# Attention block on one core: ones in every eighth column of the value tiles, and the next keys at an earlier tile count

## The chip, the core and the metric

The kernel runs on one core of a Trainium2 chip. The metric is the device time of one execution in microseconds (us): 416.04 us, the median of three runs (415.42 to 416.15). The core has a matrix engine (PE, TensorE), a vector engine (DVE, VectorE), an activation engine (ACT, ScalarE), a general engine (POOL, GpSimd) and an engine that here only issues DMAs (SP, SyncE). Each runs its own instructions in the order in which the program holds them and waits on semaphores for the others. PE writes to PSUM, eight banks of 128 x 512 floats; the other data lie in SBUF.

## The reference, cut to what matters

```python
B, S, D, H = 1, 2048, 448, 16          # Dh = 28
qkv = (x @ wqkv).reshape(B, S, 3, H, Dh).transpose(2, 0, 3, 1, 4)
q, k, v = qkv
scores = einsum("bhqd,bhkd->bhqk", q, k) * Dh ** -0.5
o = einsum("bhqk,bhkd->bhqd", softmax(scores), v)
return o.transpose(0, 2, 1, 3).reshape(B, S, D) @ wo
```

All in bfloat16. The bulk is 16 heads x 2048 x 2048 exponentials.

## The kernel before, in words

**Tiling.** The 16 heads form four groups g of four; the 2048 queries form four chunks c of 512. A pair (g, c) is a window; 16 windows run one after the other, group by group. In a window there are 16 rows of 128 keys, each with four score tiles, one a head, of 128 keys x 512 queries: 64 tiles a window, 256 a group, 1024 in all. `pos` counts the score tiles started. A head takes 32 partitions or columns (HP), of which 28 carry data. Scores are computed transposed (keys on the partitions), so that the exponentials go straight into the product with the values.

**Score tile.** `emit_S` (L865) multiplies a block of keys (KB) with the queries (QB). The stationary operand spans 64 partitions, two heads' strips: one strip of 32 holds the head's data, the other holds in KB a row of key maxima (the bound) and in QB the absolute queries, so that a bound on the scores is subtracted within the matmul. The bound makes the exponentials safe without a maximum over the scores.

**Exponentials.** Three engines share them. ACT takes two tiles at a time out of a double bank PA into PTA (L1288). DVE takes single tiles out of one of three banks PD: DU (L1069), DV (L1072), then POOL's product DG (L1075), then DVE's sum PTD (L1088). A few tiles ("g") are copied to SG by DVE (L1001) and worked off by POOL alone (L1008 to L1031); such a tile is chosen 10 to 13 rows ahead.

**Values.** `pv_op` (L1133) multiplies the 32 value columns of a head (VA) with the exponentials and adds up over the 16 rows of a window in the one bank PO. Of the 32 columns 28 are values and the last four are ones (L317, L450), so that partitions 28 to 31 of each head's strip of PO hold the softmax denominators.

**End of a window.** `finish_window` (L944): PO is copied to OSB (L953); one denominator row a head, four rows, is gathered by a DMA into DCO, 128 x 16 (L960); DVE inverts it into DRC (L962); a DMA writes it to DRAM as four rows of 512 (SCR, L963); a DMA reads each row 32 times into the 128 partitions of RRB (L965); POOL multiplies OSB by RRB into OT (L968). The last window is normalized on DVE instead, by transposes (`norm_dve`, L876). OT of all four groups goes through the output projection with WO (L789, L807, L827, L899, L1420), which has its rows laid out as the heads' strips (L445).

**First two windows.** Their first four rows run before the bound of all keys is known, with a bound from the first chunk; `task_factor` (L906) computes the ratio exp(old bound - new bound) into RR, writes eight of its rows to DRAM (SCRF, L930), broadcasts them into RRB (L931), and `finish_block` rescales the first part by them (L941).

**Work for the next group.** While group g-1 runs, its tasks are woven in. `task_K` (L509): for each chunk sc of 512 keys four matmuls (L523), an eviction into KB on DVE (L558) and a maximum (L562). Chunk sc may start from tile (g-1)*256 + sc*KSP + 2 (L519); it takes the bank PO when no window holds it, and any free bank PD from (sc+1)*KSP - UK on (L518). After all four chunks, `task_kmax` (L568) reduces the maxima (L572), builds the bound tile NK on POOL (L616), copies two strips of keys into the second KB tile (KB<-KB, L604) and writes the bound beside each head's keys (KB<-NK, four DMAs, L614). `task_Q` (L628) makes the queries of a window about one window ahead and lays them out with six DMAs (L701, L707). `task_V` (L714) makes VA and evicts it on DVE (L739).

**Order.** The order of every engine is fixed at build time by a planner in the kernel (from L1324 on). It steps through modelled time; each operation has an engine, a duration, a latency until others see it, dependencies, a priority and perhaps a tile count from which it is eligible. On PE, score matmuls for ACT come first, then those for DVE, then the value matmuls once enough rows are ready (10 at the start of a window), then the tasks. DMAs count 0.4 to 0.6 us on SP; GLAT is the modelled time from there until the broadcast RRB has landed, and so sets where in POOL's order the multiply by RRB stands. The chip then keeps that order and waits wherever a semaphore isn't there yet. The priority of the multiply and of the DMAs of the end of a window is -10, ahead of the tiles'.

Of the kernel before, what the change touches and what calls it, by code (L numbers as in the profile page):

```python
# [10 lines left out]
ALU = mybir.AluOpType  # L11
# [3 lines left out]
F32 = mybir.dt.float32  # L15
# [3 lines left out]
P = 128  # L19
H = 16  # L20
HP = 32
G = 4
HG = 4
CC = 4
QW = 512
# [57 lines left out]
def kernel(  # L83
# [7 lines left out]
    nc = tc.nc  # L91
    _, S, D = x.shape
    Dh = D // H
# [3 lines left out]
    TPC = QW // P  # L97
    SCALE = float(Dh) ** -0.5
    YSC = 128.0 / LN2 * SCALE
    GW = HG * Dh  # L100
# [12 lines left out]
    NG = 3  # L113
    GMAX = 1
    UK = 30
    KSP = 64
    PGX = 0
    GDEC = 4
    LA = 10
# [18 lines left out]
    PFIN = 0.3  # L138
    QEA = 20
    PLT = 6.0  # L140
    GLAT = 6.5
    J3 = 9
    UQ = 60
    OD = 2
# [18 lines left out]
    NF = 2  # L163
# [41 lines left out]
    def sb(shape, dt, name):  # L205
        return const.tile(shape, dt, name=name)
# [5 lines left out]
    WO = sb([P, G, D], BF16, "WO")  # L212
# [32 lines left out]
    PA = [psum.tile([P, UA * QW], F32, name=f"PA{i}") for i in range(NA)]  # L245
# [84 lines left out]
    def add(op):  # L330
        static[op.eng].append(op)
        return op
# [108 lines left out]
        add(Op("SP", 8.5, None, prio=-1995.5))  # L441

    def load_wo():
        for i in range(HG):
            nc.sync.dma_start(out=WO[HP * i:HP * i + Dh, :, :],  # L445
                              in_=bass.AP(wo.tensor, wo.offset + i * Dh * D, [[D, Dh], [HG * Dh * D, G], [1, D]]))

    def va_ones():
        for g in range(1, G):
            nc.gpsimd.memset(VA[g][:].rearrange("p j h e -> p (j h) e")[:, :, Dh:HP], 1.0)  # L450
    add(Op("POOL", 0.9, va_ones, prio=-50, elig=lambda t: pos[0] >= 8))

    def halves():
        nc.gpsimd.memset(negm[:], 0.0)
        nc.gpsimd.memset(FW[:], 0.0)
        for w in range(NF):
            cs = slice(w * HP // NF, (w + 1) * HP // NF)
            nc.gpsimd.tensor_scalar(out=negm[:, w, cs], in0=maskm[:, cs], scalar1=-1.0, scalar2=0.0, op0=ALU.mult, op1=ALU.add)
    add(Op("POOL", 0.8, halves, prio=-49, elig=lambda t: pos[0] >= 8))
    add(Op("SP", 1.7, load_wo, prio=-500, elig=lambda t: pos[0] >= 110))  # L460
    for s in a_slots + d_slots + [o_slot]:
        s.free_at = 1e18

# [250 lines left out]
    def task_V(g, jq):  # L714
        due = g * 4 * WT + jq * TPC * HG - 12 + (FB * HG * (NF - 1) if g == 0 and jq else 0)
        task = bank_task()
        early = False
        elig = at(VE + jq * 5 if g == 0 else (g - 1) * 4 * WT + jq * WT + 4)
        prio = due
        ap = lambda: bank(task)[:]  # L720

        def mm(jj):
            for cc in range(CC):
                nc.tensor.matmul(out=ap()[:, jj * GW:(jj + 1) * GW], lhsT=XT[jq][cc // 2][0:CK, cc % 2, jj * P:(jj + 1) * P],  # L724
                                 rhs=WV[:, cc, g * GW:(g + 1) * GW], start=(cc == 0), stop=(cc == CC - 1))
        ops = []
        for jj in range(TPC):
            ops.append(add(Op("PE", 0.27, (lambda jj=jj: mm(jj)), deps=(xt_done[jq] + [wvin]) if jj == 0 else [ops[-1]],
                              prio=prio + 0.001 * jj, kind="W", elig=elig, acq=acq_d(task, early, urgent=due - UV if g == 0 else (g - 1) * 4 * WT + (jq + 1) * WT + 32) if jj == 0 else None,
                              lat=0.0 if jj < TPC - 1 else PLAT)))  # L730
        o = VA[g][:, jq * TPC:(jq + 1) * TPC, :, 0:Dh]
        eng = "ACT" if early else "DVE"

        def ev_fn():
            src = ap()[:, 0:TPC * GW].rearrange("p (j h d) -> p j h d", j=TPC, d=Dh)
            if eng == "ACT":
                nc.scalar.copy(out=o, in_=src)
            else:
                nc.vector.tensor_copy(out=o, in_=src)  # L739
# [165 lines left out]

    def task_factor():  # L906
        task = bank_task()
        hh = HP // NF

        def cut():  # L910
            for w in range(NF):
                for pr in range(2):
                    nc.gpsimd.tensor_copy(out=FW[:, w * 2 + pr, w * hh:(w + 1) * hh], in_=KB[0][pr][:, QW + w * hh:QW + (w + 1) * hh])

        def mm(w):
            for i in range(HG):
# [7 lines left out]
        for w in range(NF):  # L924
# [19 lines left out]
    def finish_window(w, pvop):  # L944
# [11 lines left out]
        def rel(t):  # L956
# [5 lines left out]
        o2 = add(Op("DVE", 0.17, lambda: nc.vector.reciprocal(out=DRC[b][:], in_=DCO[b][:]), deps=o1, prio=-4000))  # L962
        o3 = add(Op("SP", 0.4, lambda: nc.sync.dma_start(out=SCR[b][:].rearrange("i (a b) -> (i a) b", b=TPC * HG),  # L963
                                                         in_=DRC[b][:]), deps=[o2], prio=-10, lat=2.0))
        o4 = [add(Op("SP", 0.6, lambda: nc.sync.dma_start(  # L965
            out=RRB[b][:], in_=bass.AP(SCR[b][:].tensor, SCR[b][:].offset, [[QW, HG], [0, HP], [1, QW]])),
            deps=[o3], prio=-10, lat=GLAT))]
        o5 = add(Op("POOL", 1.22, lambda: nc.gpsimd.tensor_tensor(out=OT[g][c][:], in0=OSB[b][:], in1=RRB[b][:], op=ALU.mult),  # L968
                    deps=o4, prio=-10, kind="n"))
# [487 lines left out]
```

## Time and profile before

| what | value |
| --- | --- |
| median of three runs | 416.04 us (415.42 to 416.15) |
| profiled execution, first to last instruction | 417.6 us |
| PE busy | 360.6 us, 86% |
| DVE busy | 378.0 us, 91% |
| ACT busy | 395.7 us, 95% |
| POOL busy | 339.2 us, 81% |
| DMA packets, bytes | 36447, 16.58 MB |

The profile shows one execution. Its own time is the span from the first to the last instruction, 417.6 us, 0.4% over the median of the runs. A group's line names the source line, the engine, the operation, what it writes and reads with shapes, the count, then busy time and mean duration of one, then the idle time just before its instructions and what ended most of that. In tables of stretches each engine has its busy microseconds and the number of its instructions; PEclk is the share of the full clock that TensorE was granted. In the timeline the idle time before an instruction and its releaser stand in brackets.

### The profile page before, as it was taken

To read this page: it belongs to the slowest core of one execution; us is meant where nothing else is said; L and a number is where in the kernel's file an instruction comes from. 1 tells how busy PE (TensorE), PEld (TensorE's weight loads), DVE (VectorE), ACT (ScalarE), POOL (GpSimd) and SP (SyncE) were. 2 spreads that over 40 slices of the span, in tenths; PEclk is the share of its full clock that TensorE was granted. 3 is DMA by queue.
4 is the path that set the end of the run, shared out by engine and by line. 5 is a ranking of instruction groups with operands and counts; after the bars stand their busy time and mean duration, and the time that the engine had idled before them with its cause. 6 is when DMAs were issued, how large, how long until landed. Compare 5 with 4: busy or idle time off the path is not lost.

```text
span 417.6 us, 7577 instructions
## 1 busy us (share of the span) xinstructions
PE 360.6 (86%) x2591; PEld 118.8 (28%) x2604; DVE 378.0 (91%) x664; ACT 395.7 (95%) x434; POOL 339.2 (81%) x365
## 2 busy tenths in 40 slices
PE   7999989898798979788598897989898898889995
PEld 4343232223123222322213222232322222222321
DVE  6996999999689999999858999999999999999884
ACT  4999999999699999999869999999999999999993
POOL 4048999687678999998877899898989989999960
PEclk9999999999799999999969999999999999999999
DMA  9351130203300001110500101000140000010112
GB/s 211 49 85 44 36 74 6 48 5 75 67 1 27 19 29 29 20 35 5 104 17 2 36 12 34 14 28 19 29 94 3 26 20 27 2 39 9 67 49 89
DMA packets 36447, 16.58 MB, mean 40 GB/s; under 512 B 28785, under 2 KB 33137, under 8 KB 36409
## 3 DMA queue, kind: packets, MB, share of 16 engines
q1 hardware_dynamic: 35800, 15.89, 16.3%
q8 instruction: 20, 0.33, 0.3%
q10 hardware_dynamic: 608, 0.22, 0.2%
q14 instruction: 19, 0.15, 0.1%
HBM read 7.44 MB, written 1.97 MB: 23 GB/s over the span
## 4 chain that ended last, share of the span: by engine, by line
ACT 52%; PE 25%; DVE 8%; issue 7%; DMA 5%; POOL 2%; SPq 1%; DVEq 0%; ACTq 0%; POOLq 0%
ACT PTA L1288 51%; PE PA L865 10%; PE PO L1133 8%; PE PD L865 3%; DMA KB<-NK 2%; DVE DU L1069 2%; DVE DV L1072 1%; DMA KB<-KB 1%; DMA WK<-in_wqkv_dram 1%; DVE PTD L1088 1%; POOL DG L1075 1%; PE PO L523 1%; DVE QB L679 1%; DVE XT L426 1%; DVE KB L550 0%
## 5 line engine op out<-in xcount | busy, mean ns | idle before, releaser
L1288 ACT ACTIVATE PTA<-PA 128x1024 bf16<-128x1024 f32 x422 | 388.3, 1190 | 9.0 <-PE PA L865 8.2
L1075 POOL TENSOR_TENSOR DG<-DV,DU 128x512 f16<-128x512 f16 x155 | 177.3, 1156 | 38.1 <-DVE DV L1072 31.8
L865 PE MATMUL PA<-QB,KB 64*128 64x512 bf16 x843 | 170.9, 384 | 42.1 <-ACT PTA L1288 39.6
L865 PEld LDWEIGHTS <-KB 64*128 64x128 bf16 x1024 | 65.7, 93 | 187.7 <-issue 173.6
L1069 DVE TENSOR_SCALAR DU<-PD 128x512 f16<-128x512 uint16 x155 | 103.1, 682 | 10.8 <-PE PD L865 10.2
L1088 DVE SCALAR_TENSOR_TENSOR PTD<-PD,DG 128x512 uint16<-128x512 f32 x155 | 104.1, 682 | 4.5 <-POOL DG L1075 4.0
L1072 DVE SCALAR_TENSOR_TENSOR DV<-PD,DU 128x512 f16<-128x512 uint16 x155 | 103.5, 683 | 0.9
L1133 PE MATMUL PO<-PTA,VA 128*32 128x512 bf16 x843 | 88.4, 396 | 0.1
L865 PE MATMUL PD<-QB,KB 64*128 64x512 bf16 x181 | 65.0, 387 | 6.3 <-DMA KB<-NK 5.4
L1133 PE MATMUL PO<-PTD,VA 128*32 128x512 bf16 x181 | 51.7, 396 | 0.3 <-issue 0.3
L1133 PEld LDWEIGHTS <-VA 128*32 128x32 bf16 x1024 | 19.4, 94 | 52.4 <-issue 52.0
L1018 POOL TENSOR_TENSOR SG<-SG,GU 128x512 f32<-128x512 f32 x26 | 30.1, 1158 | 3.3 <-DVE PTD L1088 2.5
L1014 POOL TENSOR_TENSOR GV<-GE,GU 128x512 f16<-128x512 f32 x26 | 30.1, 1157 | 2.1 <-DVE DU L1069 0.9
L1016 POOL TENSOR_TENSOR GU<-GV,GU 128x512 f16<-128x512 f16 x26 | 30.1, 1156 | 1.2 <-DVE QP L692 0.5
L1001 DVE COPY SG<-PD 128x512 f32<-128x512 f32 x26 | 17.8, 685 | 10.8 <-PE PD L865 10.5
L1008 POOL TENSOR_SCALAR GU<-SG 128x512 f16<-128x512 uint16 x26 | 16.1, 621 | 9.3 <-DVE SG L1001 7.6
L968 POOL TENSOR_TENSOR OT<-OSB,RRB 128x512 bf16<-128x512 f32 x15 | 19.1, 1271 | 3.6 <-DVE QP L692 2.2
L1031 POOL TENSOR_SCALAR PTD<-SG 128x512 uint16<-128x512 f32 x26 | 16.2, 621 | 5.1 <-DVE QP L692 3.4
L653 PE MATMUL PO<-XT,WQP 112*128 112x512 bf16 x56 | 18.8, 386 | 0.4 <-DVE KB L550 0.4
L1011 POOL TENSOR_SCALAR GE<-SG 128x512 f32<-128x512 uint16 x26 | 16.1, 621 | 2.3 <-DVE QP L692 0.4
L724 PEld LDWEIGHTS <-XT 112*128 112x128 bf16 x256 | 13.4, 98 | 11.2 <-issue 10.9
L523 PE MATMUL PO<-XT,WKP 112*128 112x512 bf16 x48 | 15.4, 385 | 0.0
(108 smaller groups left out, 189.1 us busy)
## 6 DMA issues: line engine op xcount, KB each, us to landing
RRB<-SCR SPq DMA_DIRECT2D x15, 256.0 KB
QB<-QP SPq DMA_DIRECT2D x56, 32.0 KB
KB<-NK SPq DMA_DIRECT2D x12, 128.0 KB
XS<-in_x_dram SPq DMA_DIRECT2D x3, 448.0 KB
QB<-QB SPq DMA_DIRECT2D x28, 32.0 KB
out_dram<-XS SPq DMA_DIRECT2D x2, 448.0 KB
KB<-KB SPq DMA_DIRECT2D x6, 128.0 KB
RRB<-SCRF SPq DMA_DIRECT2D x2, 256.0 KB
```

What stands on the lines that cost most here:

```text
L523: ops = chain_mm(CC, lambda cc: nc.tensor.matmul(out=ap(), lhsT=WKP[g][:, cc, :], rhs=XT[sc][cc // 2][0:CK, cc % 2, :], start=(cc == 0), s ...
L865: nc.tensor.matmul(out=ap, lhsT=KB[g % 2][i // 2][a:a + 64, j * P:(j + 1) * P], rhs=QB[w % NQB][i // 2][a:a + 64, :], start=True, stop=Tru ...
L968: o5 = add(Op("POOL", 1.22, lambda: nc.gpsimd.tensor_tensor(out=OT[g][c][:], in0=OSB[b][:], in1=RRB[b][:], op=ALU.mult), deps=o4, prio=-10 ...
L1014: g3 = add(Op("POOL", PTT, lambda: nc.gpsimd.tensor_tensor(out=GV[:], in0=GE[:], in1=GU[:], op=ALU.mult), deps=[g2], prio=prio + 2, kind=" ...
L1016: g4 = add(Op("POOL", PTT, lambda: nc.gpsimd.tensor_tensor(out=GU[:], in0=GV[:], in1=GU[:], op=ALU.mult), deps=[g3], prio=prio + 3, kind=" ...
L1018: g5 = add(Op("POOL", PST, lambda: nc.gpsimd.tensor_tensor(out=X[:], in0=X[:], in1=GU[:], op=ALU.add), deps=[g4], prio=prio + 4, kind="g", ...
L1069: p1 = add(Op("DVE", P1, lambda: nc.vector.tensor_scalar(out=DU[b][:], in0=lo, scalar1=SIG / 65536, scalar2=SIG * (SS - 0.5), op0=ALU.mult ...
L1072: p2 = add(Op("DVE", P1, lambda: nc.vector.scalar_tensor_tensor(out=DV[b][:], in0=lo, scalar=65536 * (SS - 0.5 + CE / C3), in1=DU[b][:], o ...
L1075: gq = add(Op("POOL", PTT, lambda: nc.gpsimd.tensor_tensor(out=DG[b][:], in0=DV[b][:], in1=DU[b][:], op=ALU.mult), deps=[p2], prio=n, kind ...
L1088: f = add(Op("DVE", P1, lambda: nc.vector.scalar_tensor_tensor(out=PTD[st["s"].idx][:].bitcast(U16), in0=PX[slot.idx][:], scalar=EBITS + C ...
L1133: nc.tensor.matmul(out=PO[HP * st:HP * (st + 1), :], lhsT=VA[g][:, j, st, :], rhs=r["p"][i][1](), start=first, stop=last, tile_position=(0 ...
L1288: nc.scalar.activation(out=PTA[pslot.idx][:, 0:len(ns) * QW], in_=PA[s.idx][:, 0:len(ns) * QW], func=ACT.Exp, bias=ACT_BIAS, scale=ACT_SCALE)
```

## The change

Three things. **The ones** move from the last four columns of each head's 32 to every eighth column (RS = 8): seven values, a one, seven values, a one. So PO has its denominators at partitions 7, 15, 23, ..., 127, each head's four times; the gather takes 16 rows (NR), the reciprocal is over 128 x 64, SCR is 16 x 512, and the broadcast reads 16 rows eight times each. The value evictions write runs of 7; WO has its rows spread accordingly and is loaded in seven DMAs, not four; `norm_dve` reads column 7. **The rescale factors** RR get the same layout, each of the two windows having four of each eight columns, and go from RR in SBUF straight to RRB; SCRF is gone. **Two constants of the planner**: KSP 64 to 52, GLAT 6.5 to 2.4 (and the modelled durations of the load of WO, 1.7 to 2.9, and of the reciprocal, 0.17 to 0.22).

```diff
+RS = 8
+NR = 128 // RS
...
-    KSP = 64
+    KSP = 52
...
-    GLAT = 6.5
+    GLAT = 2.4
...
-    DCO = [sb([P, TPC * HG], F32, f"DCO{i}") for i in range(2)]
-    DRC = [sb([P, TPC * HG], F32, f"DRC{i}") for i in range(2)]
+    DCW = QW * NR // P
+    DCO = [sb([P, DCW], F32, f"DCO{i}") for i in range(2)]
+    DRC = [sb([P, DCW], F32, f"DRC{i}") for i in range(2)]
...
-    SCRF = dram.tile([HG, NF, QW], F32, name="SCRF")
-    SCR = [dram.tile([HG, QW], F32, name=f"SCR{i}") for i in range(2)]
+    SCR = [dram.tile([NR, QW], F32, name=f"SCR{i}") for i in range(2)]
...
+    def cols_of(ap, w):
+        f = RS // NF
+        return ap.rearrange("p (m e) -> p m e", e=RS)[:, :, w * f:(w + 1) * f]
+
+    def va_rows(g):
+        return VA[g][:].rearrange("p j h (m e) -> p (j h m) e", e=RS)
...
-    nc.vector.memset(VA[0][:].rearrange("p j h e -> p (j h) e")[:, :, Dh:HP], 1.0)
+    nc.vector.memset(va_rows(0)[:, :, RS - 1:RS], 1.0)
...
-        for i in range(HG):
-            nc.sync.dma_start(out=WO[HP * i:HP * i + Dh, :, :],
-                              in_=bass.AP(wo.tensor, wo.offset + i * Dh * D, [[D, Dh], [HG * Dh * D, G], [1, D]]))
+        for e in range(RS - 1):
+            nc.sync.dma_start(out=WO[e::RS, :, :],
+                              in_=bass.AP(wo.tensor, wo.offset + e * D, [[(RS - 1) * D, NR], [HG * Dh * D, G], [1, D]]))
...
-        o = VA[g][:, jq * TPC:(jq + 1) * TPC, :, 0:Dh]
+        nv = TPC * HG * HP // RS
+        o = va_rows(g)[:, jq * nv:(jq + 1) * nv, 0:RS - 1]
...
-        nc.vector.reciprocal(out=dr, in_=dt[:, Dh::HP])
+        nc.vector.reciprocal(out=dr, in_=dt[:, RS - 1::HP])
...
-        d = add(Op("SP", 0.5, lambda: nc.sync.dma_start(out=SCRF[:].rearrange("i w q -> (i w) q"), in_=RR[0::hh, :]), deps=[e], prio=-10, lat=2.0))
         return [add(Op("SP", 0.6, lambda w=w: nc.sync.dma_start(
-            out=RRB[w][:], in_=bass.AP(SCRF[:].tensor, SCRF[:].offset + w * QW, [[NF * QW, HG], [0, HP], [1, QW]])),
-            deps=[d], prio=-10, lat=GLAT)) for w in range(NF)]
+            out=RRB[w][:], in_=RR[w * RS // NF::RS, None, :].to_broadcast([NR, RS, QW])), deps=[e], prio=-10, lat=GLAT)) for w in range(NF)]
...
-            out=DCO[b][:], in_=OSB[b][Dh::HP, :].rearrange("i (a b) -> i a b", b=TPC * HG)), deps=[ev], prio=-10, lat=2.6))]
-        o2 = add(Op("DVE", 0.17, lambda: nc.vector.reciprocal(out=DRC[b][:], in_=DCO[b][:]), deps=o1, prio=-4000))
-        o3 = add(Op("SP", 0.4, lambda: nc.sync.dma_start(out=SCR[b][:].rearrange("i (a b) -> (i a) b", b=TPC * HG),
+            out=DCO[b][:], in_=OSB[b][RS - 1::RS, :].rearrange("i (a b) -> i a b", b=DCW)), deps=[ev], prio=-10, lat=2.6))]
+        o2 = add(Op("DVE", 0.22, lambda: nc.vector.reciprocal(out=DRC[b][:], in_=DCO[b][:]), deps=o1, prio=-4000))
+        o3 = add(Op("SP", 0.4, lambda: nc.sync.dma_start(out=SCR[b][:].rearrange("i (a b) -> (i a) b", b=DCW),
                                                          in_=DRC[b][:]), deps=[o2], prio=-10, lat=2.0))
...
-            out=RRB[b][:], in_=bass.AP(SCR[b][:].tensor, SCR[b][:].offset, [[QW, HG], [0, HP], [1, QW]])),
+            out=RRB[b][:], in_=bass.AP(SCR[b][:].tensor, SCR[b][:].offset, [[QW, NR], [0, RS], [1, QW]])),
             deps=[o3], prio=-10, lat=GLAT))]
```

The weights of the factor matmuls (FW, negm) are cut by `cols_of` in place of halves of the 32 columns; their shapes stay.

More of the change, by code (lines that the diff above doesn't have):

```diff
@@ L443, in load_wo @@
     def load_wo():
-        for i in range(HG):
-            nc.sync.dma_start(out=WO[HP * i:HP * i + Dh, :, :],
-                              in_=bass.AP(wo.tensor, wo.offset + i * Dh * D, [[D, Dh], [HG * Dh * D, G], [1, D]]))
+        for e in range(RS - 1):
+            nc.sync.dma_start(out=WO[e::RS, :, :],
+                              in_=bass.AP(wo.tensor, wo.offset + e * D, [[(RS - 1) * D, NR], [HG * Dh * D, G], [1, D]]))
     def va_ones():
         for g in range(1, G):
-            nc.gpsimd.memset(VA[g][:].rearrange("p j h e -> p (j h) e")[:, :, Dh:HP], 1.0)
+            nc.gpsimd.memset(va_rows(g)[:, :, RS - 1:RS], 1.0)
     add(Op("POOL", 0.9, va_ones, prio=-50, elig=lambda t: pos[0] >= 8))
@@ L456, in halves @@
         for w in range(NF):
-            cs = slice(w * HP // NF, (w + 1) * HP // NF)
-            nc.gpsimd.tensor_scalar(out=negm[:, w, cs], in0=maskm[:, cs], scalar1=-1.0, scalar2=0.0, op0=ALU.mult, op1=ALU.add)
+            nc.gpsimd.tensor_scalar(out=cols_of(negm[:, w, :], w), in0=maskm[:, 0:HP // NF].rearrange("p (m f) -> p m f", f=RS // NF),
+                                    scalar1=-1.0, scalar2=0.0, op0=ALU.mult, op1=ALU.add)
     add(Op("POOL", 0.8, halves, prio=-49, elig=lambda t: pos[0] >= 8))
-    add(Op("SP", 1.7, load_wo, prio=-500, elig=lambda t: pos[0] >= 110))
+    add(Op("SP", 2.9, load_wo, prio=-500, elig=lambda t: pos[0] >= 110))
     for s in a_slots + d_slots + [o_slot]:
@@ L730, in task_V @@
                               lat=0.0 if jj < TPC - 1 else PLAT)))
-        o = VA[g][:, jq * TPC:(jq + 1) * TPC, :, 0:Dh]
+        nv = TPC * HG * HP // RS
+        o = va_rows(g)[:, jq * nv:(jq + 1) * nv, 0:RS - 1]
         eng = "ACT" if early else "DVE"
         def ev_fn():
-            src = ap()[:, 0:TPC * GW].rearrange("p (j h d) -> p j h d", j=TPC, d=Dh)
+            src = ap()[:, 0:TPC * GW].rearrange("p (n e) -> p n e", e=RS - 1)
             if eng == "ACT":
@@ L907, in task_factor @@
         task = bank_task()
-        hh = HP // NF
         def cut():
@@ L912, in cut @@
                 for pr in range(2):
-                    nc.gpsimd.tensor_copy(out=FW[:, w * 2 + pr, w * hh:(w + 1) * hh], in_=KB[0][pr][:, QW + w * hh:QW + (w + 1) * hh])
+                    nc.gpsimd.tensor_copy(out=cols_of(FW[:, w * 2 + pr, :], w),
+                                          in_=KB[0][pr][:, QW:QW + HP // NF].rearrange("p (m f) -> p m f", f=RS // NF))
         def mm(w):
```

## The prediction, made before the changed kernel ran

> **What bounds the kernel now.** Read first the page: its head, the share of each engine, the slices of the clock, and the costliest group.
>
> ```profile
> span 417.6 us, 7577 instructions
> PE 360.6 (86%) x2591; PEld 118.8 (28%) x2604; DVE 378.0 (91%) x664; ACT 395.7 (95%) x434; POOL 339.2 (81%) x365
> PEclk9999999999799999999969999999999999999999
> L1288 ACT ACTIVATE PTA<-PA 128x1024 bf16<-128x1024 f32 x422 | 388.3, 1190 | 9.0 <-PE PA L865 8.2
> ```
>
> ACT is the bound: 95% busy, nearly all of it the exponentials of L1288, which were idle 9.0 us, 8.2 of them waiting for score matmuls (L865). The granted clock dips in two slices only. So the second view is the table of busy time by stage, cut where the groups of heads change (four groups, so three changes); columns: stretch, its length, PE, PEld, DVE, ACT, POOL, clock, DMA share, GB/s.
>
> ```profile
> 91.00:125.00 34.00, 28.79 (x186) 8.15 (x179) 28.72 (x51) 30.18 (x34) 25.63 (x27) 0.90 0.21 44
> 195.00:220.00 25.00, 19.08 (x132) 5.09 (x130) 18.07 (x32) 19.96 (x22) 19.67 (x20) 0.86 0.25 51
> 298.00:322.00 24.00, 20.96 (x155) 7.07 (x155) 23.06 (x41) 24.00 (x28) 22.35 (x23) 1.00 0.25 54
> 322.00:408.00 86.00, 76.83 (x528) 23.99 (x534) 80.86 (x137) 86.00 (x95) 76.96 (x77) 1.00 0.09 29
> ```
>
> In the last two stretches ACT is busy all the time, the third change of group included. In the first it lacks 34.00 - 30.18 = 3.82 us, in the second 25.00 - 19.96 = 5.04 us. Third view, the waits inside these two stretches, the first two lines from the first change, the others from the second:
>
> ```profile
> ACT PTA L1288 <- PE PA L865: 3.8, 5, 2.1
> PE PD L865 <- DMA KB<-NK: 2.0, 1, 2.0
> ```
>
> ```profile
> ACT PTA L1288 <- PE PA L865: 4.4, 2, 3.8
> PE PD L865 <- DMA KB<-NK: 3.4, 1, 3.4
> ```
>
> PE, which issues in order, stands before one score matmul of the next group until the copies of the bound row into the keys (KB<-NK) have landed. That lasts 2.0 and 3.4 us, yet ACT loses 3.82 and 5.04. The clock says why (the first change, by the microsecond):
>
> ```profile
> 110.00:111.00 1.00, 0.82 (x3) 0.28 (x4) 0.18 (x1) 0.00 (x0) 0.00 (x0) 0.51 0.23 62
> 117.00:118.00 1.00, 1.00 (x16) 0.31 (x12) 0.93 (x3) 0.81 (x2) 1.00 (x2) 1.00 0.00 0
> ```
>
> After the hole PE runs at about half clock until the microsecond from 117, and ACT waits for it again. The Trainium skill, "TensorE: Matmul & The Clock Gate", section "HAM oscillation", sets the gap to avoid at over about 3.4 us; by it the 2.0 us gap should have cost no clock, and that change of group would lose its longest wait of 2.1 us in place of 3.82, making the gain 1.7 us smaller. The row shows half clock after 2.0 us; the measurement decides.
>
> Where the late copies come from, second change, from the timeline:
>
> ```profile
> 197.66 0.74 DVE L558 TENSOR_SCALAR KB<-PO,onescol 128x512 bf16<-128x512 f32 x1
> 201.33 0.38 POOL L616 TENSOR_SCALAR NK<-maskm,KMAX 128x128 bf16<-128x128 bf16 x1
> 203.15 1.97 SPq L614 DMA_DIRECT2D KB<-NK  x3
> 209.48 0.60 PE L865 MATMUL PD<-QB,KB 64*128 64x512 bf16 x1 [3.44 <-DMA KB<-NK]
> ```
>
> The fourth key chunk is evicted at 197.66, the bound follows at 201.33, the copies at 203.15, and PE resumes at 209.48: 11.8 us from chunk to use, begun too late.
>
> **The change, part by part.**
>
> *Next keys sooner (KSP 64 to 52).* Chunk sc of the next group may start from score tile 52 sc + 2 of the current group, not 64 sc + 2: the fourth from 158, not 194. It also needs a bank, in practice PO between two windows. Where these gaps lie, counted by the score matmuls (L865) issued up to a time, with the two events that frame the gap before the last in the second group:
>
> ```profile
> 0.00:169.10 169.10, 82.78 (x405) 25.91 (x406) 0.98 0.24 50
> 0.00:184.00 184.00, 90.73 (x444) 28.45 (x444) 0.98 0.23 48
> 0.00:194.70 194.70, 96.24 (x475) 30.38 (x476) 0.98 0.22 46
> ```
>
> ```profile
> 169.07 0.68 DVE L953 COPY OSB<-PO 128x512 f32<-128x512 f32 x1
> 180.31 0.60 PE L653 MATMUL PO<-XT,WQP 112*128 112x512 bf16 x2
> ```
>
> Score tiles of this group count from 256. PO is evicted at tile 405 - 256 = 149, a query task still uses it at 180.31, and by 184.00 tile 188 is reached: 158 falls inside. Today's 194 misses it and waits for the gap at 194.7, tile 219. The fourth chunk therefore moves one gap ahead, by up to 194.7 - 169.1 = 25.6 us; 9 of the gap's 39 tiles pass first, 9/39 of 14.9 us, so about 22 us sooner, against copies late by 3.4. The chain that it issues (two KB<-KB, four KB<-NK, on SP) goes ahead of that gap's query copies, which are for a window not yet due and have most of a window to spare. No instruction is added: four matmuls, an eviction, a reduction per chunk as before.
>
> So both holes close, as at the third change, where ACT lost nothing: 3.82 + 5.04 = **8.86 us** off. Bounds: 0 if the wait stays, 8.86 as all the idle of those stretches.
>
> *Broadcast as 16 rows, planned 4.1 us sooner (GLAT 6.5 to 2.4).* The first view is the broadcast's groups, the second SP's and POOL's timeline around two broadcasts, the third the DMA share of two half microseconds of the later one, and of a store with 128 rows.
>
> ```profile
> L965 SPq DMA_DIRECT2D RRB<-SCR x15: 532/573/587, 55.4 to 393.1; - x15
> L968 POOL TENSOR_TENSOR OT<-OSB,RRB x15: 1266/1271/1277, 63.3 to 400.8; 128x512 bf16<-128x512 f32 x15
> ```
>
> ```profile
> 99.62 0.59 SPq L965 DMA_DIRECT2D RRB<-SCR  x1
> 106.72 1.27 POOL L968 TENSOR_TENSOR OT<-OSB,RRB 128x512 bf16<-128x512 f32 x1 [0.30 <-DVE QP L692]
> 348.42 0.57 SPq L965 DMA_DIRECT2D RRB<-SCR  x1
> ```
>
> ```profile
> 350.40:350.90 0.50, 0.49 (x3) 0.17 (x2) 0.50 (x2) 0.50 (x2) 0.35 (x1) 1.00 0.26 102
> 352.40:352.90 0.50, 0.50 (x10) 0.25 (x10) 0.50 (x2) 0.50 (x2) 0.44 (x2) 1.00 0.06 21
> 393.00:394.00 1.00, 0.96 (x6) 0.30 (x4) 0.55 (x2) 1.00 (x2) 1.00 (x2) 1.00 1.01 401
> ```
>
> Four rows go out at 102 GB/s with a quarter of the DMA engines busy, the last bytes some 4.4 us after the issue (352.8 - 348.42). The store shows 401 GB/s on all. 256 KB takes 2.57 us at the first rate and 0.65 at the second; 16 rows lie between, and I take the second, since a quarter share with four rows looks like one engine a row. Landing then comes 4.4 - 1.9 = 2.5 us after the issue. The Trainium skill, "DMA: Bandwidth & Descriptors", section "Why a DMA increments its semaphore by 16 and not by 1", gives it as a rule: a DMA runs on the largest number of engines, up to 16, that divides the slowest dimension of both sides; 4 agrees with the trace, 16 no row of before shows.
>
> Today the multiply starts 7.9, 7.1 and 7.7 us after the issue (first, tight, last). Placed 4.1 sooner, it finds the rows there: 7.1 - 4.1 - 2.5 = 0.5 us to spare in the tight one. POOL would wait with DG (L1075) behind it, and DVE's third pass and its bank behind that. I put 0.4 us of jitter on the end for it; bounds, 0 and the rival below.
>
> *The rest of the chain and the evictions.*
>
> ```profile
> L962 DVE RECIPROCAL DRC<-DCO 128x16 f32<-128x16 f32 x15 | 3.6, 243 | 0.0
> L1069 DVE TENSOR_SCALAR DU<-PD 128x512 f16<-128x512 uint16 x155 | 103.1, 682 | 10.8 <-PE PD L865 10.2
> L739 DVE CAST VA<-PO 128x448 bf16<-128x448 f32 x12 | 7.4, 615 | 0.0
> L814 DVE CAST XS<-PO 128x448 bf16<-128x448 f32 x4 | 2.4, 602 | 0.0
> L445 SPq DMA_DIRECT2D WO<-in_wo_dram x4: 384/394/427, 53.5 to 54.9; - x4
> ```
>
> The reciprocal takes 64 columns, not 16: (682 - 243) / (512 - 16) = 0.89 ns a column, 48 more are 43 ns, times 15 is 0.64 us of DVE. A tile costs DVE three passes of 682 ns, 2.05 us; so 0.3 tiles go over to ACT, which makes a pair in 86.00 / 95 = 0.91 us: 0.14 us. The value evictions (L739) write runs of 7 where they wrote 28. Runs of 28 cost 615 ns against 602 for one run of 448 (L814), so I take 0; at worst, doubled, 16 (these 12 and 4 into PD) x 0.615 = 9.8 us of DVE, 4.8 tiles, 2.2 us of ACT. Output weights come in seven loads, not four: 3 x 0.394 = 1.2 us of SP, ahead of the first broadcast (55.4), whose multiply at 63.3 covers it, or else 1.2 us of POOL once. The gather and its write carry 32 KB for 8, 0.24 us more at 102 GB/s, in the same chain, with the spare time above; on 16 rows it can also be shorter. The rescale factors skip one trip through DRAM, early and off the path: 0. The ones' memsets write as many elements, during the loads: 0. The final normalization reads another column of the same transpose: 0.
>
> Sum against the profiled span: -8.86 + 0.14 + 0.4 + 0.3 (my allowance for small waits left at a change of group) = -8.0, 409.6 us. The runs' median is 416.04 against that span of 417.6, a factor 0.9963: **408.0 us**.
>
> **The rivals.**
>
> *One hole stays.* Something else due at the change is next in line, most likely the first window's queries, whose copies start in the last gap. Against: at the third change their copies left in time. For: moving the fourth chunk forward fills an earlier gap, and a query task may slip. A wait of 2 us costs 3.82 through the clock. With the smaller saving of 5.04 and 0.8 of costs: 413.4 of span, 411.8 us.
>
> *The keys aren't sooner.* If a window's accumulation takes PO first, the fourth chunk misses the gap and lands where it is today: 417.6 + 0.8, 416.8 us; with the costs at zero, 416.0. The counts speak against it: 158 is 9 tiles into a gap of 39.
>
> *Slower: the multiply waits at the head of POOL.* If the broadcast still lands after 4.4 us, a multiply placed 4.1 us sooner waits 0.8 (first window), 1.4 (tight) or 0.9 us (last): about 1.0 each, 15 us on POOL. It passes to DVE, to the tiles that the value matmuls take in order, and so to ACT: 417.6 - 8.86 + 0.8 + 15 = 424.5, 422.9 us. It turns the sign once more than 8.06 / 15 = 0.54 us a window reaches ACT. POOL's 19% of idle and the buffered tiles speak against all of it getting there; the DMA share against its beginning.
>
> **How the numbers follow.** Forecast 0.75, at 408.0. One hole stays 0.12, at 411.8. Keys not sooner 0.05, at 416 to 416.8. Slower 0.08. The range runs from 405.4 (no costs, 407.2, and DVE, idle 5.28 + 6.93 us in the two stretches, taking 4 more tiles of ACT's 0.45 us each) to 412.5 (one hole stays, with 0.7 more from evictions): it leaves out the last two cases and a little of the first. A measurement of this kernel tells 0.2%, 0.8 us, from no change, so "same" is 415.2 to 416.9. Faster 0.87, same 0.05, slower 0.08.
>
> **What would show it.** ACT busy throughout the stretches of the first two changes of group; no wait of L865 for KB<-NK; no dip in the clock's slices; the fourth chunk's matmuls one gap earlier; the broadcast above 300 GB/s for under a microsecond; POOL not idle before OT; the cast of VA still near 615 ns. Wrong if: a hole moves to another load (queries, weights), POOL waits for RRB, or DVE's share of tiles falls by more than two, each 0.45 us.

## The result, and the profile after

The changed kernel takes 414.56 us (median of nine runs, 413.50 to 415.49), the kernel before 417.73 us (median of nine, 415.42 to 419.69, the first three among them): a ratio of 0.9933, 95% interval 0.9908 to 0.9958. So it is faster by 0.67%, where the prediction had 1.9%, and the time lies outside the predicted range (405.4 to 412.5).

The page of the changed kernel: head, engines, clock, costliest group.

```profile
span 413.3 us, 7565 instructions
PE 360.2 (87%) x2591; PEld 120.9 (29%) x2602; DVE 382.9 (93%) x664; ACT 395.2 (96%) x434; POOL 340.5 (82%) x365
PEclk9799999999999999999999999999999999999998
L1295 ACT ACTIVATE PTA<-PA 128x1024 bf16<-128x1024 f32 x422 | 387.7, 1170 | 1.0 <-PE PA L875 0.9
```

The exponentials, still 422 pairs, wait 0.9 us for score matmuls in all, where they waited 8.2. Both dips at the changes of group are gone from the clock's row, and a new one stands in the second slice. The stretches around the first two changes of group, same columns as in the prediction:

```profile
91.00:125.00 34.00, 30.26 (x232) 9.15 (x232) 33.45 (x57) 33.56 (x37) 31.59 (x34) 1.00 0.17 39
195.00:220.00 25.00, 22.40 (x160) 7.39 (x160) 24.40 (x43) 25.00 (x28) 21.89 (x23) 1.00 0.11 30
```

ACT is busy 33.56 of 34 and 25.00 of 25 us: the two holes of the prediction are closed. What took the gain back is seen when one asks when the exponentials begin and end. The group's row of ACT gives shortest/median/longest in ns, then the first and the last start in us; before, then after:

```profile
L1288 ACT ACTIVATE PTA<-PA x422: 632/1206/1294, 11.3 to 408.2; 128x1024 bf16<-128x1024 f32 x141
```

```profile
L1295 ACT ACTIVATE PTA<-PA x422: 681/1174/1294, 16.1 to 403.9; 128x1024 bf16<-128x1024 f32 x141
```

From first to last start it was 408.2 - 11.3 = 396.9 us and is 403.9 - 16.1 = 387.8: 9.1 us off. But the first exponential starts 4.8 us later. What follows the last start is 9.4 us in both. -9.1 + 4.8 = -4.3 us, the difference of the two spans (417.6 and 413.3). So the whole shortfall lies in the first 16 us. There, in the kernel before (first the group's row of the memsets, then the timeline with DVE's copies, POOL's last memset and the first score matmul):

```profile
L450 POOL MEMSET VA<- x3: 316/317/322, 4.7 to 5.2; 128x256 bf16 x3
```

```profile
5.44 0.39 DVE L379 COPY WKP<-WK 112x448 bf16<-112x448 bf16 x1 [0.68 <-DMA WK<-in_wqkv_dram]
5.50 0.20 POOL L455 MEMSET FW<- 128x128 bf16 x1
5.80 0.69 DVE L426 COPY XT<-PD 112x1024 bf16<-112x1024 bf16 x1
...
10.26 0.61 PE L865 MATMUL PA<-QB,KB 64*128 64x512 bf16 x2
```

and in the changed one, with the first key matmuls on PE too, and the clock (the column before the last two) by stretch:

```profile
L459 POOL MEMSET VA<- x3: 1247/1547/1559, 4.6 to 6.6; 128x256 bf16 x3
```

```profile
5.25 3.19 DVE L388 COPY WKP<-WK 112x448 bf16<-112x448 bf16 x1 [0.77 <-DMA WK<-in_wqkv_dram]
8.02 0.30 POOL L464 MEMSET FW<- 128x128 bf16 x1
8.37 0.67 DVE L435 COPY XT<-PD 112x1024 bf16<-112x1024 bf16 x1
...
9.09 1.01 PE L532 MATMUL PD<-XT,WKP 112*128 112x512 bf16 x2 [3.16 <-DVE XT L435]
...
15.68 0.39 PE L875 MATMUL PA<-QB,KB 64*128 64x512 bf16 x2
```

```profile
9.00:10.00 1.00, 0.91 (x3) 0.35 (x3) 0.37 (x2) 0.00 (x0) 0.00 (x0) 0.50 1.00 200
12.00:15.00 3.00, 3.00 (x26) 2.75 (x25) 1.91 (x8) 2.30 (x4) 0.00 (x0) 0.50 0.28 20
```

Read it downward. POOL's three memsets of ones (L459), as many elements as before but one in eight, are recorded with some 1.5 us each in place of 0.32; the records overlap, and from the first start to the last end they take 3.51 us in place of 0.82. DVE's copy of the key weights (L388, the first group's WKP), which stands beside them, takes 3.19 us in place of 0.39 and ends 2.6 us later (8.44 against 5.83). The transposed input behind it on DVE is late, PE stands still for 3.16 us, and when it starts the granted clock is half, from 9 to 15 us. The first score matmul starts at 15.68 in place of 10.26, 5.4 us later: 2.6 are the late copy, and the other 2.8 fall in the six microseconds at half clock. The first exponential wins 0.6 of that back, which leaves the 4.8. The copy ends 0.12 us after POOL's last memset in the row (8.02 + 0.30 = 8.32), and 0.13 us after it in the kernel before (5.70).

Theory A: the strided memsets hold up DVE's copy, and that and the clock cost the 4.8 us; without them the change would give about the forecast. Its rivals: B, something else at the start (the order of the loads, DVE's own strided memset) makes it late; and, for the gain, C, the holes closed through the rest of the change and not through the earlier keys.

### The profile page after: what moved, and what is told of

Same layout as the page of the kernel before. It is cut to its first block, busy times and chain, and to the rows that moved or that the text cites. A ratio compares the mean times of both kernels' runs of the same rounds, so it can differ in the third digit from the quotient of the medians.

```text
span 413.3 us, 7565 instructions
## 1 busy us (share of the span) xinstructions
PE 360.2 (87%) x2591; PEld 120.9 (29%) x2602; DVE 382.9 (93%) x664; ACT 395.2 (96%) x434; POOL 340.5 (82%) x365
## 3 DMA queue, kind: packets, MB, share of 16 engines
HBM read 6.91 MB, written 2.33 MB: 22 GB/s over the span
## 4 chain that ended last, share of the span: by engine, by line
ACT 36%; DVE 28%; PE 14%; POOL 9%; issue 6%; DMA 4%; SPq 1%; DVEq 0%; POOLq 0%; ACTq 0%
ACT PTA L1295 36%; DVE PTD L1095 7%; DVE DU L1076 7%; DVE DV L1079 7%; PE PA L875 5%; POOL DG L1082 5%; PE PO L1140 3%; DMA RRB<-SCR 2%; POOL GV L1021 1%; DVE SG L1008 1%; PE PD L875 1%; DMA WK<-in_wqkv_dram 1%; POOL OT L975 1%; PE PD L817 1%; DVE QB L672 1%
## 5 line engine op out<-in xcount | busy, mean ns | idle before, releaser
L875 PE MATMUL PA<-QB,KB 64*128 64x512 bf16 x843 | 168.9, 380 | 36.4 <-ACT PTA L1295 33.4
L875 PEld LDWEIGHTS <-KB 64*128 64x128 bf16 x1024 | 64.6, 93 | 176.9 <-issue 169.2
L1140 PE MATMUL PO<-PTA,VA 128*32 128x512 bf16 x843 | 86.7, 386 | 0.2
L875 PE MATMUL PD<-QB,KB 64*128 64x512 bf16 x181 | 65.9, 377 | 3.0 <-DVE PTD L1095 1.3
L1015 POOL TENSOR_SCALAR GU<-SG 128x512 f16<-128x512 uint16 x26 | 16.1, 617 | 7.2 <-DVE SG L1008 3.3
L1018 POOL TENSOR_SCALAR GE<-SG 128x512 f32<-128x512 uint16 x26 | 16.1, 618 | 2.1
L1038 POOL TENSOR_SCALAR PTD<-SG 128x512 uint16<-128x512 f32 x26 | 16.1, 619 | 1.5 <-PE PD L875 0.6
L733 PE MATMUL PO<-WV,XT 112*128 112x112 bf16 x192 | 15.5, 214 | 0.9 <-DVE QB L672 0.5
```

The costliest lines, as they stand in the source:

```text
L875: nc.tensor.matmul(out=ap, lhsT=KB[g % 2][i // 2][a:a + 64, j * P:(j + 1) * P], rhs=QB[w % NQB][i // 2][a:a + 64, :], start=True, stop=Tru ...
L1140: nc.tensor.matmul(out=PO[HP * st:HP * (st + 1), :], lhsT=VA[g][:, j, st, :], rhs=r["p"][i][1](), start=first, stop=last, tile_position=(0 ...
```

## The experiments

### The start: b_strided

The kernel before, with three strided memsets on POOL ahead of its own.

```diff
+            nc.gpsimd.memset(VA[g][:].rearrange("p j h (m e) -> p (j h m) e", e=8)[:, :, 7:8], 1.0)
+        for g in range(1, G):
```

> The kernel before, with three memsets added on POOL in front of its own: ones in every eighth column of VA for groups 1 to 3, as the changed kernel writes them; what they write is overwritten later, and every other instruction and its order stay. Theory A (the changed kernel loses 4.85 us at the start because these memsets, 1.14 us each from start to start where the old ones took 0.25, hold up DVE's copy of the padded key weights, and PE cools down in the hole that follows): the copy of WKP takes about 3 us in place of 0.39, the first exponential starts near 16 us in place of 11.3, the time rises by 4.5 to 5.5 us (ratio 1.010 to 1.013). Rival B (the start was late for another reason, the loads or the strided memset on DVE): the copy stays at 0.4 us and the time within 0.2%.

Measured: 421.79 us, ratio 1.0089 (1.0054 to 1.0123) to the kernel before beside it (417.81), so 4.0 us more, a little under theory A's band of 1.010 to 1.013; DVE's timeline and ACT's group row:

```profile
4.89 4.34 DVE L379 COPY WKP<-WK 112x448 bf16<-112x448 bf16 x1
```

```profile
L1290 ACT ACTIVATE PTA<-PA x422: 634/1218/1293, 16.3 to 411.5; 128x1024 bf16<-128x1024 f32 x141
```

The copy takes 4.34 us and the first exponential starts at 16.3, with nothing else changed. A holds and B falls: the memsets alone make the late start. The copy also lasts past the contiguous memsets that follow the strided ones: it ends at 9.23, 0.14 us after the last of eight POOL memsets in a row (9.09).

### What the price follows: m_steps

The kernel before with KSP 52 and three memsets of 256 elements on POOL, writing every second, every fourth and every eighth element.

```diff
+            nc.gpsimd.memset(VA[g][:].rearrange("p j h e -> p (j h e)")[:, 0:256 * 2 ** g].rearrange("p (n e) -> p n e", e=2 ** g)[:, :, 0:1], 1.0)
+        for g in range(1, G):
```

> The kernel before with KSP 52 and three memsets added on POOL in front of its own, each of 256 single bf16 elements: one in every second, one in every fourth, one in every eighth element. If the price is the distance, the first takes about 0.25 us from start to start like the contiguous ones, the last 1.14, the middle between; if it is the number of separate runs, all three take 1.14. Theory A in both cases: DVE's copy of WKP ends about 0.4 us after the last of the memsets, and the first exponential is late by the time the memsets add or more.

One execution took 411.22 us. The group's row:

```profile
L450 POOL MEMSET VA<- x3: 388/680/1345, 4.6 to 5.4; 128x256 bf16 x3
```

388, 680 and 1345 ns for 256 elements at steps of 2, 4 and 8 (4, 8 and 16 bytes), against 317 ns for the ones of the kernel before, which stand in runs of four. The price follows the distance between elements; the extent does not set it, since those runs of four are spread over as many columns as the elements at a step of eight. The first exponential starts at 14.8: the copy of the weights lasted 2.90 us and again ended 0.14 us after the last memset of the row (7.82 and 7.68).

### Without the memsets in the way: a_ones_late and a_wkp_act

First the changed kernel with the ones of groups 1 to 3 written some 11 us later, by a POOL operation on the first group's queries.

```diff
-            nc.gpsimd.memset(va_rows(g)[:, :, RS - 1:RS], 1.0)
-    add(Op("POOL", 0.9, va_ones, prio=-50, elig=lambda t: pos[0] >= 8))
+            nc.gpsimd.tensor_scalar(out=va_rows(g)[:, :, RS - 1:RS], in0=QB[1][0][:, 0:S // RS].rearrange("p (n o) -> p n o", o=1),
+                                    scalar1=0.0, scalar2=1.0, op0=ALU.mult, op1=ALU.add)
...
+    add(Op("POOL", 3.5, va_ones, prio=-50, deps=[qev[(0, 1, i)][0] for i in range(2)]))
```

> The changed kernel, with the ones of groups 1 to 3 written on POOL from 16 us on, after the queries of the second window are laid out, where POOL is idle; all other instructions keep their order. Theory A: the copy of WKP is back at 0.4 us, the first exponential at 11.3 to 11.6 us, and the time falls by 4.4 to 4.9 us against the changed kernel: ratio to the kernel before 0.981 to 0.984 (about 410). Rival B: the start stays late and the ratio stays near that of the changed kernel, 0.993.

Measured: 411.80 us, ratio 0.9851 (0.9814 to 0.9889). The weight copy takes 0.49 us and the first exponential starts at 11.2. Not all of the gain comes; theory A had 0.981 to 0.984. The group's row of DVE's bounds on the queries (L688), POOL's timeline, and ACT's wait:

```profile
L688 DVE TENSOR_SCALAR QB<-QP,KPART x8: 340/345/1307, 9.6 to 16.1; 32x512 bf16<-32x512 bf16 x8
```

```profile
15.82 3.97 POOL L459 TENSOR_SCALAR VA<-QB 128x256 bf16<-128x256 bf16 x3 [10.55 <-DVE QB L688]
```

```profile
ACT PTA L1296 <- PE PA L876: 1.2, 1, 1.2
```

The strided writes now stand beside another DVE operation from SBUF to SBUF, and one of its eight takes 1307 ns in place of 345; ACT waits once, 1.2 us. A part of the cost moved with the writes; the rest of the 2.1 us to the next run was not followed up.

Second, the changed kernel with its weight copy on ACT, the memsets left where they are.

```diff
-        eng = "DVE" if nm == "k" else WQE
+        eng = WQE
```

> The changed kernel with one instruction moved: the copy of the first key weights into WKP runs on ACT, not on DVE; the strided memsets stay where they are. Theory A, with the hold-up between POOL and DVE alone: ACT's copy takes about 0.57 us, the matmuls of the first keys start near 6.6 us and the time is 3.5 to 4.9 us under the changed kernel, ratio 0.982 to 0.985 (ACT has one copy more, and later DVE copies may still meet the last memset). Rival A2 (the memsets slow every engine's access to that memory): ACT's copies take over 1 us and most of the loss stays, ratio above 0.989.

Measured: 409.68 us (409.56 to 409.94), ratio 0.9804 (0.9767 to 0.9841), a little better than theory A's 0.982 to 0.985. The timeline while the three memsets run (POOL's group spans 4.64 to 8.17):

```profile
5.42 0.73 DVE L435 COPY XT<-PD 112x1024 bf16<-112x1024 bf16 x1
6.07 0.41 DVE L435 COPY XT<-PA 112x512 bf16<-112x512 bf16 x1
...
5.03 0.56 ACT L389 COPY WKP<-WK 112x448 bf16<-112x448 bf16 x1 [2.56 <-DMA WK<-in_wqkv_dram]
```

```profile
L1295 ACT ACTIVATE PTA<-PA x422: 680/1204/1294, 10.9 to 399.0; 128x1024 bf16<-128x1024 f32 x141
```

The same copy on ACT takes 0.56 us, and DVE's copies out of PSUM take 0.73 and 0.41 as before (0.69 and 0.42), all beside the same memsets. What POOL's writes hold up is DVE going from SBUF to SBUF. The Trainium skill, "SBUF — State Buffer", section "Who interferes with whom", has this as a rule: DVE and GpSimd have one pair of ports in common, and whoever takes it first keeps it for a whole instruction; DVE needs it in its two-port modes, which copies can enter, while ACT never waits. The rows agree on who is held up (3.19 us beside 0.56). They add that the hold can outlast one instruction: in each of the runs above with the copy on DVE beside POOL's memsets it ended 0.12 to 0.14 us after the last memset of the row. So does the kernel before, and the next run, where the weights come earlier: its copy, beside contiguous memsets alone, takes 1.03 us (4.78 to 5.81, the last memset ending at 5.68).

### What closed the holes: b_ksp52 and a_wkp_ksp64

The kernel before with the earlier keys alone:

```diff
-    KSP = 64
+    KSP = 52
```

> The kernel before with KSP at 52 alone. Theory A (the two holes at the changes of group are closed by the earlier keys and by nothing else of the change): no wait of the score matmuls for KB<-NK, ACT busy throughout the stretches of the changes, no dip in the clock after 20 us, the time 7 to 9 us under the kernel before: ratio 0.978 to 0.983. Rival C (the 16-row broadcast, which leaves the DMA engines free sooner, closes them): a wait of a microsecond or more stays at one change at least, and the ratio is 0.99 or more.

Measured: 407.55 us (407.53 to 408.31), ratio 0.9756 (0.9719 to 0.9793), better than theory A's 0.978 to 0.983.

```profile
91.00:125.00 34.00, 29.35 (x224) 10.94 (x219) 32.61 (x56) 34.00 (x39) 31.61 (x32) 1.00 0.07 19
195.00:220.00 25.00, 22.04 (x160) 6.89 (x156) 24.69 (x44) 25.00 (x28) 23.16 (x24) 1.00 0.08 22
```

```profile
L1288 ACT ACTIVATE PTA<-PA x421: 827/1200/1303, 11.2 to 397.0; 128x1024 bf16<-128x1024 f32 x140, 128x512 bf16<-128x512 f32 x1
```

ACT is full in both stretches and 397.0 - 11.2 = 385.8 us lie between its first and last exponential, 11.1 less than before (of which one pair, 0.9 us, has gone to DVE). One constant gives more than the whole change. The changed kernel, which has it too, evicts its fourth key chunk one gap earlier, as the prediction had it (197.66 in the kernel before):

```profile
179.11 0.74 DVE L567 TENSOR_SCALAR KB<-PO,onescol 128x512 bf16<-128x512 f32 x1
```

The other side: the changed kernel with the weight copy on ACT and the keys as before.

```diff
-    KSP = 52
+    KSP = 64
```

> The changed kernel with the WKP copy on ACT, so without the loss at the start, and with KSP back at 64: what the rest of the change is worth without the earlier keys. Theory A: the waits for KB<-NK come back at the first two changes of group with dips of the clock, ACT loses 5 to 9 us there, and the ratio to the kernel before is 0.995 to 1.005. Rival C (the 16-row broadcast frees the DMA engines and brings the keys sooner by itself): ACT loses under 3 us there and the ratio is under 0.990.

Measured: 410.11 us, ratio 0.9837 (0.9813 to 0.9862).

```profile
91.00:125.00 34.00, 29.44 (x219) 9.93 (x221) 33.18 (x58) 33.77 (x38) 28.78 (x30) 1.00 0.19 42
195.00:220.00 25.00, 21.89 (x153) 6.82 (x152) 24.71 (x43) 25.00 (x28) 23.64 (x25) 1.00 0.25 53
```

```profile
PE PD L875 <- DMA KB<-NK: 0.5, 1, 0.5
```

The holes are gone here too, with 0.5 us left of the matmul's waits of 2.0 and 3.4. So C is right as well: the rest of the change, with the order that the planner makes of it, closes them without the earlier keys. Either is enough; the gains do not add. The trace narrows it down. The fourth chunk still comes in the last gap, after PO was copied out at 94.80, but less time passes from its eviction until PE goes on. At the first change, before and then here:

```profile
97.87 0.74 DVE L558 TENSOR_SCALAR KB<-PO,onescol 128x512 bf16<-128x512 f32 x1
110.18 0.61 PE L865 MATMUL PD<-QB,KB 64*128 64x512 bf16 x1 [1.99 <-DMA KB<-NK]
```

```profile
98.51 0.74 DVE L567 TENSOR_SCALAR KB<-PO,onescol 128x512 bf16<-128x512 f32 x1
108.34 0.39 PE L875 MATMUL PD<-QB,KB 64*128 64x512 bf16 x1 [0.48 <-DMA KB<-NK]
```

That is 9.8 us in place of 12.3. Which piece of the rest shortens it (the broadcast's fewer microseconds on the DMA engines, or the order of SP's DMAs) was not taken apart.

### The multiply's place: a_wkp_glat65, b_ksp52_glat24, a_wkp_glat36

The changed kernel with the weight copy on ACT and the old GLAT:

```diff
-    GLAT = 2.4
+    GLAT = 6.5
```

> The changed kernel with the WKP copy on ACT and GLAT back at 6.5, so that POOL's multiply by RRB stands 4.1 us later in its order. Theory E (the earlier multiply is worth nothing and costs nothing): within 0.3% of the kernel with GLAT 2.4 (ratio to the kernel before 0.9804), POOL's waits for RRB (3.1 us in the changed kernel) gone. Rival F (those waits are part of the 2.1 us by which that kernel is slower than the kernel before with KSP 52 alone, 0.9756): the ratio falls to 0.975 to 0.978.

Measured: 419.73 us, ratio 1.0070 (1.0048 to 1.0092), which neither theory expected. The timeline of the place:

```profile
88.73 1.02 PE L662 MATMUL PD<-XT,WQP 112*128 112x512 bf16 x4 [0.71 <-DVE PTD L1095]
...
93.80 1.17 SPq L716 DMA_DIRECT2D QB<-QP  x2
...
96.27 0.61 PE L875 MATMUL PA<-QB,KB 64*128 64x512 bf16 x4 [0.27 <-DMA QB<-QP]
...
96.77 1.94 ACT L1295 ACTIVATE PTA<-PA 128x1024 bf16<-128x1024 f32 x2 [10.06 <-PE PA L875]
```

It is one hole, and not at the broadcast: a query task has slipped. Its matmuls run at 88.73 us, its copies are issued up to 93.80, and the next window's first scores wait for them. By 79.0 us this kernel had issued 12 query matmuls, the one with GLAT 2.4 had 16. That is the prediction's rival of a query task that slips, at 10 us. The planner set this order; why this constant tips it was not tried.

Next the prediction's slower rival by itself: four rows as before, keys earlier, and the multiply placed sooner.

```diff
-    KSP = 64
+    KSP = 52
...
-    GLAT = 6.5
+    GLAT = 2.4
```

> The kernel before with the earlier keys (KSP 52, measured alone at 407.55 us) and, of the rest of the change, only the planner's constant GLAT 2.4: the multiply OT stands some 4 us sooner in POOL's order, while the broadcast still reads four rows, whose last bytes landed 4.1 to 5.2 us after the issue. It tests the prediction's slower rival by itself. Theory K (the sooner multiply is harmless even with the late rows, because POOL's waits lie in its idle time): POOL waits for RRB about 1 us in most of the 15 windows, 10 to 15 us in all, and the time stays at 407 to 409.5 us, ratio 0.976 to 0.982 to the kernel before. Theory L (the rival: each wait reaches ACT through DVE's third pass): 415 to 422 us, with waits of L865's tiles on ACT at the ends of windows. Theory M (the 2.1 us between this kernel with KSP 52 and the changed kernel with its weight copy on ACT come from the sooner place of the multiply): 409.0 to 410.0 us, with 422 pairs on ACT in place of 421.

Measured: 432.47 us, ratio 1.0358 (1.0331 to 1.0384), 24.9 us over the same kernel with GLAT 6.5. The waits, and one of them in the timeline (the number in brackets is the wait, then its releaser):

```profile
POOL OT L968 <- DMA RRB<-SCR: 17.1, 9, 2.9
DVE PTD L1088 <- POOL DG L1075: 27.4, 26, 5.3
PE PD L865 <- DVE PTD L1088: 19.9, 27, 3.3
ACT PTA L1288 <- PE PA L865: 16.8, 22, 3.3
```

```profile
162.74 1.26 POOL L968 TENSOR_TENSOR OT<-OSB,RRB 128x512 bf16<-128x512 f32 x1 [2.33 <-DMA RRB<-SCR]
...
165.15 0.69 DVE L1088 SCALAR_TENSOR_TENSOR PTD<-PD,DG 128x512 uint16<-128x512 f32 x1 [2.00 <-POOL DG L1075]
...
165.89 0.58 PE L865 MATMUL PD<-QB,KB 64*128 64x512 bf16 x1 [2.30 <-DVE PTD L1088]
...
167.53 2.01 ACT L1288 ACTIVATE PTA<-PA 128x1024 bf16<-128x1024 f32 x2 [2.75 <-PE PO L1133]
```

```profile
163.00:167.50 4.50, 2.19 (x14) 0.43 (x13) 2.50 (x6) 1.79 (x2) 3.24 (x4) 0.74 0.00 0
167.50:171.00 3.50, 3.50 (x23) 0.59 (x19) 3.46 (x7) 2.95 (x3) 3.05 (x4) 0.50 0.21 54
```

POOL waits 2.33 us for the rows, DVE's third pass 2.00 for POOL, PE 2.30 for the bank that it frees, ACT 2.75 for PE; then the clock is at half. That is theory L, and beyond its number of 415 to 422 us. Over the whole run DVE's third pass waits 27.4 us for POOL and PE 19.9 us for the bank, against 2.4 and 0.9 us with GLAT 6.5. Nine waits of POOL, 17.1 us, go with 24.9 us of the kernel, more than they last; PE's pauses and the half clock behind them are the way that this place shows. POOL's idle time does not cover a wait at its head, because the tiles behind it are the ones that the others need.

Last, the changed kernel with the weight copy on ACT and a planned landing near the measured one:

```diff
-    GLAT = 2.4
+    GLAT = 3.6
```

> The changed kernel with its weight copy on ACT (409.68 us) and GLAT 3.6 in place of 2.4, near the 3.3 us that the broadcast of 16 rows took from its issue to its landing. Theory N (the time depends little on the planned landing while no query task slips; the multiply's place costs nothing): 408.8 to 410.2 us, 422 pairs on ACT, no wait of POOL for RRB in the profile. Theory O (the planner's order is chaotic: any other constant may move a query task past its window, as GLAT 6.5 did with a hole of 10.1 us on ACT): anything up to 420 us, and then with one wait of ACT of several microseconds for score tiles while the queries of the next window are late. Theory P (a multiply that does not wait frees DVE and POOL for two more tiles): 407.5 to 408.8 us, 421 pairs on ACT.

Measured: 409.00 us (408.88 to 409.16), ratio 0.9799 (0.9777 to 0.9821).

```profile
L1295 ACT ACTIVATE PTA<-PA x421: 1018/1259/1293, 10.9 to 396.8; 128x1024 bf16<-128x1024 f32 x141
```

One pair fewer than with 2.4, and its exponentials end as early as those of the kernel with KSP 52 alone (396.8 against 397.0). The median lies 0.7 us under the one with 2.4, but the intervals overlap: P points the right way and is not proven. POOL's waits for RRB are small in both (0.2 us here, 0.5 with 2.4), and the pair fewer is the planner's doing, since the split of the tiles is fixed when the kernel is built. What still parts it from 407.55 lies after the last exponential: 407.1 - 396.8 = 10.3 us against 405.7 - 397.0 = 8.7. Why the end is longer was not tried.

### The longer reciprocal: b_ksp52_rec64

The kernel before with KSP 52 and reciprocals over 64 columns, 48 of them filled with ones and not used.

```diff
-    DCO = [sb([P, TPC * HG], F32, f"DCO{i}") for i in range(2)]
-    DRC = [sb([P, TPC * HG], F32, f"DRC{i}") for i in range(2)]
+    DCO = [sb([P, 4 * TPC * HG], F32, f"DCO{i}") for i in range(2)]
+    DRC = [sb([P, 4 * TPC * HG], F32, f"DRC{i}") for i in range(2)]
```

> The kernel before with KSP 52, and with the reciprocal over 128 x 64 floats, as the changed kernel has it, of which 16 columns are used; the order of all instructions stays (two small memsets more on DVE at the start). Theory G (the reciprocals, 544 ns for 243, 15 times, 4.5 us of DVE, are part of the 2.1 us between the changed kernel without its memset loss and KSP 52 alone): the time rises by 0.5 to 2 us over that of KSP 52 alone, ratio 0.977 to 0.980. Rival H (they lie in DVE's slack): within 0.4 us, ratio 0.975 to 0.9765.

Measured: 407.69 us, ratio 0.9783 (0.9757 to 0.9809); its span is 405.7 us, that of the kernel without it. The ratio by itself would fall into theory G's band, but only because the kernel before ran at 416.71 us beside it, not at 417.81; time and span stand with H.

```profile
L964 DVE RECIPROCAL DRC<-DCO 128x64 f32<-128x64 f32 x15 | 8.1, 543 | 0.0
```

15 x (543 - 243) = 4.5 us more of DVE, at no cost that shows: they lie in its idle time.

## Why the prediction was wrong, step by step

**The step that failed** is "The ones' memsets write as many elements, during the loads: 0." The count was right and the cover was not. The price is the step: 1247 to 1559 ns at a step of eight elements, 317 ns before, and 3.51 us for the three in place of 0.82. And what lies beside them is not only loads: the weight copy of L379, at 5.44 us in the timeline of before, is on the chain to the first exponential. Put alone into the kernel before they cost 4.0 us (interval 2.3 to 5.1); in the changed one the first exponential starts 4.8 us later.

**With that step taken out the ratio agrees, in part by luck.** The forecast is 408.0 / 416.04 = 0.9807 of the kernel before; the changed kernel with its weight copy on ACT measured 0.9804 (0.9767 to 0.9841). But two parts are off and cancel: KSP 52 alone took 10.3 us off the kernel before beside it (417.81), not 8.86, and the rest of the change added 2.1 (407.55 to 409.68), not 0.84. In microseconds it is 409.68, not 408.0. The prediction's factor 0.9963 from span to time is no property of the kernel: every recorded run takes 1.7 to 2.1 us more than its own span (415.08 for 413.3), so the profile of 417.6 us belongs to an execution of about 419.4 us (an estimate from these differences), one of the slower ones before. In the ratio that slip nearly drops out.

**The holes** were forecast at -8.86 us; from the first to the last exponential 9.1 us went. The place, the waits and the clock were read rightly. The cause was half right: the fourth chunk did move one gap ahead and the earlier keys close the holes alone (407.55), but the rest of the change closes them too (410.11 with KSP 64), so the part credited to one edit was there twice.

**The clock.** The prediction kept the row's half clock after a 2.0 us gap against the rule of the Trainium skill ("TensorE: Matmul & The Clock Gate", section "HAM oscillation") of about 3.4 us. PE's 3.16 us at the start and its 2.30 us in the run of the sooner multiply are under that as well, and the rows behind them show 0.50. The measurement decides again.

**The broadcast** goes faster as forecast, on 16 rows, but less so. The best half microsecond of the last one, issued at 392.15:

```profile
393.65:394.15 0.50, 0.46 (x4) 0.18 (x2) 0.50 (x1) 0.50 (x2) 0.42 (x2) 1.00 0.89 319
```

It moves 319 GB/s, where four rows had 102 and the prediction took 401. The median from issue to landing is 3.3 us; the forecast had 2.5. So there was nothing to spare, and POOL waited:

```profile
POOL OT L975 <- DMA RRB<-SCR: 3.1, 4, 1.3
```

That is 3.1 us in four multiplies. What it cost at the end, 0.4 us in the sum, no run shows by itself: with the weight copy on ACT the same order waits once, 0.5 us.

**The slower rival** did not come, for the reason given, the faster rows. Its mechanism was right, and its 15 us too small: with four rows it costs 24.9. (Its waits of 0.8 and 0.9 us in the first and last window should be 0.6 and 0.8 by its own figures, which leaves "about 1.0 each" as it is.)

**The reciprocal** was mis-sized: the prediction took 43 ns for 48 more columns from the slope of a tensor_scalar; it is 543 - 243 = 300 ns, 6.3 ns a column. It costs nothing here. **The value evictions** in runs of seven take 614 ns, 615 before, as forecast.

## What to carry to other kernels

A cost of zero needs two rows: one that shows the duration of the new form, stride included, and one that shows what runs beside it; here, in the first microseconds, what ran beside it was the critical chain. A constant that places a waiting instruction in an in-order queue should not lie below the measured latency: 0.9 us below it (2.4 against 3.3) cost little, 2 us below it (2.4 against 4.4) cost 25 us. How far above is best is not shown; 6.5 stood in the fastest kernel. And when two edits of one change remove the same wait, each may do it alone: KSP 52 alone, 407.55 us, beat the whole change.

## What the runs showed of the hardware that was not expected

- A memset's time follows the distance between the elements written: 256 elements of two bytes took POOL 317 ns in runs of four, and 388, 680 and up to 1559 ns one by one at steps of two, four and eight.
- POOL's memsets held up a DVE copy from SBUF to SBUF from 0.39 to 3.19 and 4.34 us, until 0.12 to 0.14 us after the last memset of the row, and neither ACT's copy (0.56 us) nor DVE's copies out of PSUM.
- A reciprocal on DVE costs 6.3 ns a column of 128 floats, seven times the 0.89 ns that the prediction read from a tensor_scalar.
